# The opening of a Fourier-mixing and feed-forward kernel: some loads moved to GpSimd's queue, half a weight fold moved, one column sent and fetched half a step earlier

## The chip, the cores and the metric

The kernel runs on one core of a Trainium2 chip. A core has TensorE (matrix products, PE in the profile, PEld for its weight loads), VectorE (DVE), ScalarE (ACT), GpSimd (POOL) and SyncE (SP), each with its own instruction order, and 16 DMA engines that serve transfers issued by SyncE, ScalarE or GpSimd. An engine waits for another by semaphores. The metric is the device time of one execution in microseconds; the median of three runs before the change is 1947.78 us (1946.93 to 1948.93).

## The reference

Two stages, all in float32:

```python
def _attn_ref(x):                      # x: (8, 3008, 256)
    X = np.fft.fft(x, axis=1)
    X = np.fft.fft(X, axis=2)
    return X.real

def _moe_ref(x, w_in, w_out):          # x: (24064, 256), w_in: (256, 2048), w_out: (2048, 256)
    h = x @ w_in
    g = h * np.cos(h)
    return g @ w_out
```

The real part of a two-dimensional Fourier transform of each batch is the input of a feed-forward layer whose activation is h cos(h).

## The kernel before, in words

**The transform along the sequence.** 3008 is split as 47 x 64. `load_x` (L146) brings one batch of x into four tiles `xp`, p = 0 to 3, of eight columns i (the index of 64) together with their eight mirror columns. Each p takes four transfers, two of 32 and two of 16 partitions: the columns as they stand (L154), 8 KB in a piece, and the mirror columns in reverse order (L161), 1 KB in a piece. For p = 0 the mirror of column 0 is row 32, which is a transfer of its own (L159) beside the other seven (L156). `fold` (L248) forms sums and differences along d, and a small copy (L259) puts two border columns in place. For the first batch the folds are VectorE's and the small copies GpSimd's, into two buffers `xf` whose lower halves GpSimd clears at the start (L238). `first_half` (L274 to L291) multiplies by the table `L`, ScalarE copies the result out (L308), `store_z` (L348) writes it to DRAM and `load_z` (L358) reads it back in another layout. `second_half` (L372) multiplies by twiddles from the table `BJ` in groups g of four j; ScalarE copies the result to `pq` (L384, L387 in the first group).

**The transform along d is folded into the weights.** `weights` (L438) multiplies blocks q of 512 columns of w_in (`wr`, raw) by the cosine and sine table `CS`, two products for the two halves of the rows. VectorE copies the sums to `WC` and `WS` (L449). The first row of `WS` is used as a per-feature factor: `send_wn` (L479) writes it to DRAM (`wd`) and has GpSimd clear the row afterwards (L480), and `load_wn` (L483) fetches it as four columns of `wn`, 128 x 4 elements of 4 bytes. Block 0 takes another way (L458 to L472). `combine_w2` (L521) forms four sums and differences of blocks of w_out (`w2`) in `VX`, on GpSimd.

**The steady loop.** For 8 batches, 6 groups and 8 pairs of feature blocks there is a step t; a step has two half steps k = 2t and 2t + 1. A half step seeds a PSUM tile H from `nb` and `wn` (`seed`, L536), adds two products by WC and WS (`mm1`, L555), and goes through ScalarE and VectorE by `act_e`, `dve_h`, `act_round`, `dve_frac`, `act_sin`, `dve_g` (L567 to L597). Once a step, GpSimd forms sums `S` (L613 to L620), and seven products by w2 and VX follow (`mm2`, L646), five half steps behind the first. The next batch's transform is woven into the loop.

**The opening** is what comes before the loop runs full. Python order is issue order on every engine (the schedule is manual), and the waits are added between them. A dummy product by `keep_busy` (L502) runs on TensorE before the first data come. Then come the loads, the first batch's folds and products in the order p = 1, 2, 0, 3, the first weight folds, the first group of the second half, and half steps k = 0 to 4, in which the other weight blocks are folded between the products. Nearly all loads are SyncE's; ScalarE issues three x loads and a few small ones. Transfers of SyncE and ScalarE share eight completion semaphores in turn, so the issue of one waits until the one eight places earlier has landed. In half step 0 the first two units take their product by WC and a product with one row (`seed_first`, L542), instead of a seed by ScalarE; then `spread_nb` (L403, L404) fills `nb`:

```python
            if k == 0:
                for h in (cur, nxt):
                    mm1(h, 0)
                    seed_first(h)
                    act_e(h)
                spread_nb(0)
            if k < AHEAD - 1:
                mm1(cur, 1)
            if k == 0:
                weights(0, 1, pw=pw[0], both=(1,))
```

Of the kernel before, what the change touches and what calls it, by code (L numbers as in the profile page):

```python
# [18 lines left out]
ND = 256  # L19
# [8 lines left out]
NX = 96  # L28
# [86 lines left out]
def kernel(  # L115
# [7 lines left out]
    nc = tc.nc  # L123
    NB = x.shape[0]
    L_np, B_np, CS_np = _consts()
    L_dr = nc.inline_tensor(L_np, name="dft_L")
    ident_dr = nc.inline_tensor(np.eye(128, dtype=np.float32), name="ident")
    B_dr = nc.inline_tensor(B_np, name="dft_B")
    CS_dr = nc.inline_tensor(CS_np, name="dft_CS")

    x_r = x.rearrange("b (s2 s1) d -> b s2 s1 d", s1=64)
# [9 lines left out]
    xs = {}  # L141

    def take_x(b, p):
        xs[b, p] = spool.tile([128, XP * ND], FP, tag="xp", bufs=4, name="xp")

    def load_x(b, p, others=(nc.sync, nc.sync)):  # L146
        if (b, p) not in xs:
            take_x(b, p)
        xt = xs[b, p]
        xv = xt.rearrange("r (i d) -> r i d", d=ND)  # L150
        i0 = XP * p
        for r0, r1, at, by, other in ((0, 32, 0, 3, others[0]), (31, 47, 2, 6, others[1])):
            lo, hi = xv[at:NX:by], xv[at + by // 2 : NX : by]
            nc.sync.dma_start(out=lo, in_=x_r[b, r0:r1, i0 : i0 + XP, :])  # L154
            if p == 0:
                other.dma_start(  # L156
                    out=hi[:, 1:XP], in_=x_r[b, r0:r1, 63 : 64 - XP : -1, :]
                )
                other.dma_start(out=hi[:, 0:1], in_=x_r[b, r0:r1, 32:33, :])  # L159
            else:  # L160
                other.dma_start(  # L161
                    out=hi, in_=x_r[b, r0:r1, 64 - i0 : 64 - i0 - XP : -1, :]
                )
# [18 lines left out]
            in_=CS_dr.ap().rearrange("(i p) d -> p i d", p=128),  # L182
        )

    def load_w(q):
        nc.sync.dma_start(
            out=wr[q][:, 0:1024].rearrange("p (i f) -> p i f", i=2),
            in_=moe_w_in[:, 512 * q : 512 * q + 512].rearrange("(i p) f -> p i f", p=128),
        )

    def load_bj(c0, c1):
        nc.sync.dma_start(out=BJ[:, c0:c1], in_=B_dr.ap()[:, c0:c1])

    def load_ident():
        nc.sync.dma_start(out=ident, in_=ident_dr.ap())

    def load_w2(f0, f1):
        nc.sync.dma_start(
            out=w2.rearrange("p (q c) -> p q c", c=ND)[:, 2 * f0 : 2 * f1],
            in_=moe_w_out.rearrange("(q p) c -> p q c", p=128)[:, 2 * f0 : 2 * f1],  # L200
        )

    load_x(0, 1, (nc.scalar, nc.scalar))
    nc.sync.dma_start(out=L, in_=L_dr.ap())
    load_x(0, 2, (nc.scalar, nc.sync))
    load_x(0, 0)
    load_x(0, 3)
    load_cs()
    load_w(0)
    WC = cpool.tile([128, NDFF], FP, tag="WC", name="WC")  # L210
    WS = cpool.tile([128, NDFF], FP, tag="WS", name="WS")
    wn = cpool.tile([128, 16], FP, tag="wn", name="wn")
# [186 lines left out]
    def spread_nb(g):  # L399
        pq, nb = ready[0, g]  # L400
        T = _width(g)
        pn = borrow("pn") if g else psum("pn", "M")
        nc.tensor.matmul(pn[:, 0:T], lhsT=ones, rhs=pq[0:1, T : 2 * T], start=True, stop=True)  # L403
        nc.scalar.copy(out=nb[:, 0:T], in_=pn[:, 0:T])  # L404
# [30 lines left out]
    def weights(e, n, tag="M", pw=None, both=(0, 1)):  # L435
        pw = pw or psum("pw", tag)
        for i in both:
            nc.tensor.matmul(  # L438
                pw,
                lhsT=CS[:, 256 * i + 128 * e : 256 * i + 128 * e + 128],  # L440
                rhs=raw(n, i),
                start=(i == 0),
                stop=(i == 1),
            )
        return pw
# [30 lines left out]
    def send_wn(n):  # L476
        row = WS[0:1, 512 * n : 512 * n + 512]
        wds[n] = dpool.tile([1, 512], FP, tag="wd", bufs=3, name="wd")
        nc.scalar.dma_start(out=wds[n], in_=row)  # L479
        nc.gpsimd.memset(row, 0.0)  # L480

    def load_wn(n, eng=nc.sync):
        eng.dma_start(  # L483
            out=wn[:, 4 * n : 4 * n + 4], in_=wds[n].rearrange("o (k p) -> (o p) k", p=128)
        )
# [13 lines left out]
    def keep_busy(k, tag, n):  # L499
        pd = psum("pd", tag)  # L500
        for i in range(k):
            nc.tensor.matmul(  # L502
                pd[:, 0:n],
                lhsT=VX[:, 0:128],
                rhs=VX[:, 0:n],
                start=i == 0,
                stop=i == k - 1,
            )
# [55 lines left out]
    def act_e(h):  # L564
        T = h.s.T
        h.ew = spool.tile([128, 256], FP, tag="ew", bufs=2, name="ew")
        nc.scalar.mul(out=h.ew[:, 0:T], in_=h.H[:, 0:T], mul=2.0)  # L567
# [225 lines left out]
    both = nc.sync, nc.scalar  # L793
    copy_v = nc.vector.tensor_copy
    keep_busy(1, "H", 512)
    keep_busy(1, "H", 512)
    keep_busy(1, "M", 512)
    for p in (1, 2, 0, 3):
        for c in (2 * p, 2 * p + 1):
            chunk(c)  # L800
            first_half(0, c)
        store_z(0, p, 0, 4, both if p == 3 else (nc.sync, nc.sync))
        if p == 1:
            load_bj(0, 512)
        elif p == 2:
            load_w(1)
    load_z(0, 0, 0, 4)
    load_z(0, 1, 0, 4, both)
    fold_weights(1, 0, "H", copy_v)
# [1 line left out]
    take_wn(0)  # L811
    fold_weights(1, 1, "M", copy_v)
    send_wn(1)
    load_w2(0, 2)
    load_w(2)
    load_w(3)
    load_w2(2, 4)
    load_wn(1)
    for p in (1, 2, 0, 3):
        store_z(0, p, 4)  # L820
    load_bj(512, 1024)
    for half in range(2):
        load_z(0, half, 4)
    load_w2(4, 6)
# [37 lines left out]
    for k in range(2 * n + LAG):  # L862
        t, u = divmod(k, 2)
        d, v = divmod(k - LAG, 2)
        cur, prev, old, nxt = unit(k), unit(k - 1), unit(k - 2), unit(k + 1)
        done = step(d)
        full = step(d if v else d - 1, True)
        if cur:
            if k % (2 * per) == 0:
                todo = transform(cur.s.b + 1) if cur.s.b + 1 < NB else {}  # L870
            if k >= AHEAD:
                mm1(cur, 0)
                act_e(cur)
            if k == 0:
                for h in (cur, nxt):
                    mm1(h, 0)
                    seed_first(h)
                    act_e(h)
                spread_nb(0)
            if k < AHEAD - 1:  # L880
                mm1(cur, 1)
            if k == 0:
                weights(0, 1, pw=pw[0], both=(1,))
        pair = None if u else pairs.pop(t, None)
        if pair:
            b, c = pair
            pz = [first_half(b, c, borrow("pz"))]
        if old:
            dve_g(old)
            if old.u:  # L890
                sums(old.s)
        if pair:
            pz.append(first_half(b, c + 1, borrow("pz", 1)))
        pm = clear_middle() if u and t in middles else None
        if done:
            order = (0, 1, 5, 4, 3, 2, 6) if done is steps[-1] else range(7)
            mm2(done, 4 * v, 4 * v + 3, order)
        if pm is not None:
            middle(pm)
        if full and full is not steps[-1]:  # L900
            take_m(full, 1 if v else 3, nc.vector)
        if nxt and 0 < k < AHEAD - 1:
            seed(nxt)
        if prev:
            act_round(prev)
        if pm is not None:
            nc.scalar.copy(out=zm[64:128], in_=pm)
        if pair:
            keep_z(b, c, pz[0])
        if nxt and k >= AHEAD - 1:  # L910
            seed(nxt)
        if full and full is not steps[-1]:
            take_m(full, 0 if v else 2, nc.scalar)
        if prev:
            dve_frac(prev)
        if k + 1 in range(2, AHEAD):
            mm1(nxt, 0)
            act_e(nxt)
        if k in (1, 2, 3, 4):
            pw.append(weights(*((1, 2), (0, 2), (1, 3), (0, 3))[k - 1]))  # L920
        copy_small()
        if prev:
            act_sin(prev)
        if pair:
            keep_z(b, c + 1, pz[1])
            patch_z(b, c)
            patch_z(b, c + 1)
        if cur and k >= AHEAD - 1:
            mm1(cur, 1)
        if done and v == 0:  # L930
            mm2(done, 3, 4, order)
        if cur:
            dve_h(cur)
        if k in (1, 2, 3, 4, 5):
            e, q = ((0, 1), (1, 2), (0, 2), (1, 3), (0, 3))[k - 1]
            keep_weights(e, q, pw[k - 1], copy_v)
        if k in (3, 5):
            send_wn((k + 1) // 2)
        if k in (5, 7):
            load_wn((k - 1) // 2, nc.scalar)  # L940
        if u == 0:
            continue
        for i in range(6):
            s = step(t - 4 - i, True)
            if s:
                combine_m(s, i)
        for sg, lag in ((0, 8), (1, 10)):
            s = step(t - lag, True)
            if s:
                store_out(s, sg)  # L950
        for call in opening.pop(t, ()):
            call[0](*call[1:])
        for call in todo.pop(t % per, ()):
            call[0](*call[1:])
# [31 lines left out]
```

## Time and profile before

| What | Value |
|---|---|
| Median of three runs | 1947.78 us |
| Profiled execution, time | 1947.23 us |
| Profiled execution, span | 1945.4 us |
| TensorE busy | 1932.7 us, 99% of the span |
| VectorE, ScalarE, GpSimd busy | 1462.6, 1505.6, 1400.1 us |
| Folds of x on VectorE, first batch (L248) | 16, 676 ns each |
| First and last fold's set begin | 6.85 us, 17.82 us |
| First product of the first stage, end of that stage on TensorE | 7.95 us, 21.49 us |
| Second stage's first product (L372) | 27.89 us |
| First product with S (L646) | 47.03 us |
| TensorE gapless from | 53.05 us |
| GpSimd's first clear of xf | 0.73 us, two of them 1.84 us |

"L12" is line 12 of the kernel. A group of the profile shows line, engine, operation, what is written and read, count, busy time and mean, and then the idle time of that engine before it with what ended it. A row of the timeline begins with start and length in microseconds. Waits give the total, how many and the longest. A weight load or product is recorded as two passes per instruction in float32, so one product counts as two. "SPq", "ACTq" and "POOLq" are an engine's instruction queue, where DMAs are issued. The granted clock of TensorE is 1.00 at full speed. Idle time of an engine that nobody waits for costs nothing.

### The profile page before, as it was taken

The page shows a single profiled execution, that of the slowest core. Times are in us where ns is not written, and L with a number is a line of the kernel's source. Part 1 is how long each engine was busy: PE and PEld are TensorE (multiplying, and loading weights), DVE is VectorE, ACT ScalarE, POOL GpSimd, SP SyncE. Part 2 cuts the span into 40 slices and gives each one's busy share as a digit, 9 for nine tenths or more (in the row PEclk, how much of TensorE's full clock was granted, in tenths as well). Part 3 has the DMA queues.
Part 4 walks back from the last instruction along what each step waited for, and adds up shares of the span by engine and source line. Part 5 has one row for each costly group of instructions (what it writes and reads, how often), then busy time and mean ns, then how long its engine had stood idle before and what let it go on. Part 6 is the DMA issues. An engine that isn't in the chain of part 4 may idle for free.

```text
span 1945.4 us, 29495 instructions
## 1 busy us (share of the span) xinstructions
PE 1932.7 (99%) x9228; PEld 1682.0 (86%) x9228; DVE 1462.6 (75%) x2537; ACT 1505.6 (77%) x3439; POOL 1400.1 (72%) x1594
## 2 busy tenths in 40 slices
PE   8999999999999999999999999999999999999998
PEld 5888898888988889888898888988889888898887
DVE  4677777777777777777777777777777777788787
ACT  3777778777787777877778787788777887778775
POOL 3777757787677766787668776677767777666765
PEclk9999999999999999999999999999999999999999
DMA  8411122012220223112230112312113111100001
GB/s 212 119 28 39 28 58 72 18 39 40 54 62 19 42 41 77 36 23 40 40 90 21 39 26 41 88 24 40 24 40 87 24 39 28 39 22 16 12 14 31
DMA packets 177373, 89.09 MB, mean 46 GB/s; under 512 B 103825, under 2 KB 174271, under 8 KB 175554
## 3 DMA queue, kind: packets, MB, share of 16 engines
q1 hardware_dynamic: 174404, 86.05, 19.6%
q10 hardware_dynamic: 2814, 1.16, 0.3%
q8 instruction: 75, 1.23, 0.3%
q14 instruction: 80, 0.66, 0.1%
HBM read 49.90 MB, written 37.28 MB: 45 GB/s over the span
## 4 chain that ended last, share of the span: by engine, by line
PE 97%; DMA 2%; SPq 0%; DVE 0%; ACTq 0%; issue 0%; POOL 0%; ACT 0%; POOLq 0%; DVEq 0%
PE M L646 58%; PE H L555 33%; PE pz L277 3%; PE pb L372 2%; DMA xp<-in_x_dram 1%; DMA wn<-wd 0%; PE pw L438 0%; DMA z<-zd 0%; DMA wd<-WS 0%; DMA zd<-zs 0%; SPq L348 0%; PE pz L274 0%; PE pm L329 0%; SPq L154 0%; DVE cb L714 0%; ACTq L161 0%
## 5 line engine op out<-in xcount | busy, mean ns | idle before, releaser
L613 POOL TENSOR_TENSOR S<-r 128x512 f32<-128x512 f32 (+1 forms) x383 | 475.6, 1242 | 443.5 <-DVE r L597 392.0
L587 DVE SCALAR_TENSOR_TENSOR r<-r,H 128x512 f32<-128x512 f32 (+1 forms) x768 | 518.9, 676 | 195.2 <-ACT r L583 168.6
L593 ACT ACTIVATE r<-r 128x512 f32<-128x512 f32 (+1 forms) x768 | 477.0, 621 | 240.2 <-DVE r L587 235.5
L597 DVE SCALAR_TENSOR_TENSOR r<-H,r 128x512 f32<-128x512 f32 (+1 forms) x768 | 519.1, 676 | 131.5 <-ACT r L593 91.6
L646 PE MATMUL M<-S,VX 128*128 128x256 f32 (+1 forms) x2304 | 615.2, 376 | 0.0
L646 PEld LDWEIGHTS M<-S,VX 128*128 128x128 f32 x2304 | 435.4, 190 | 71.3 <-issue 22.7
L555 PE MATMUL H<-pq,WC 128*128 128x256 f32 (+1 forms) x1536 | 453.6, 377 | 1.4 <-ACT H L536 1.3
L555 PE MATMUL H<-pq,WS 128*128 128x256 f32 (+1 forms) x1536 | 451.3, 375 | 0.0
L583 ACT ACTIVATE r<-H 128x512 f32<-128x512 f32 (+1 forms) x768 | 447.7, 583 | 0.2 <-DVE H L571 0.2
L571 DVE TENSOR_TENSOR H<-ew,H 128x256 f32<-128x256 f32 (+1 forms) x768 | 324.9, 423 | 133.3 <-PE H L555 74.7
L646 PE MATMUL M<-r,w 128*128 128x256 f32 (+1 forms) x1536 | 387.6, 375 | 0.0
L567 ACT ACTIVATE ew<-H 128x256 f32<-128x256 f32 (+1 forms) x768 | 287.7, 375 | 123.2 <-PE H L555 119.1
L536 ACT ACTIVATE H<-nb,wn 128x256 f32<-128x256 f32 (+1 forms) x766 | 366.0, 478 | 2.7 <-DMA wn<-wd 1.8
L646 PEld LDWEIGHTS M<-r,w 128*128 128x128 f32 x1536 | 300.5, 196 | 27.5 <-issue 0.5
L555 PEld LDWEIGHTS H<-pq,WS 128*128 128x128 f32 x1536 | 290.3, 190 | 34.4 <-issue 1.5
L555 PEld LDWEIGHTS H<-pq,WC 128*128 128x128 f32 x1536 | 279.6, 190 | 45.6 <-ACT H L536 9.3
L619 POOL TENSOR_TENSOR S<-S,r 128x256 f32<-128x256 f32 (+1 forms) x383 | 276.0, 721 | 30.0
L620 POOL TENSOR_TENSOR S<-r,S 128x256 f32<-128x256 f32 (+1 forms) x383 | 275.3, 719 | 30.0
L646 PE MATMUL M<-S,w 128*128 128x256 f32 (+1 forms) x768 | 225.2, 375 | 0.0
L646 PE MATMUL M<-r,VX 128*128 128x256 f32 (+1 forms) x768 | 225.1, 375 | 0.0
L646 PEld LDWEIGHTS M<-S,w 128*128 128x128 f32 x768 | 150.5, 196 | 14.6
L646 PEld LDWEIGHTS M<-r,VX 128*128 128x128 f32 x768 | 145.8, 190 | 14.6
(76 smaller groups left out, 918.0 us busy)
## 6 DMA issues: line engine op xcount, KB each, us to landing
out_dram<-ob SPq DMA_DIRECT2D x724, 32.0 KB
xp<-in_x_dram SPq DMA_DIRECT2D x54, 256.0 KB
zd<-zs SPq DMA_DIRECT2D x56, 192.0 KB
z<-zd SPq DMA_DIRECT2D x28, 384.0 KB
xp<-in_x_dram SPq DMA_DIRECT2D x55, 128.0 KB
nb<-nd SPq DMA_DIRECT2D x39, 128.0 KB
wr<-in_moe_w_in_dram SPq DMA_DIRECT2D x4, 512.0 KB
w<-in_moe_w_out_dram SPq DMA_DIRECT2D x4, 512.0 KB
```

What stands on the lines that cost most here:

```text
L536: nc.scalar.activation(out=h.H[:, 0:T], in_=s.nb[:, 0:T], func=AF.Copy, bias=0.25, scale=wn[:, f : f + 1])
L555: nc.tensor.matmul(h.H[:, 0:T], lhsT=W[:, 128 * f : 128 * f + 128], rhs=s.pq[:, e * T : e * T + T], start=False, stop=True, skip_group_che ...
L567: nc.scalar.mul(out=h.ew[:, 0:T], in_=h.H[:, 0:T], mul=2.0)
L571: nc.vector.tensor_tensor(out=h.H[:, T : 2 * T][:, ::-1], in0=h.ew[:, 0:T], in1=h.H[:, 0:T], op=ALU.subtract)
L583: nc.scalar.activation(out=r, in_=y, func=AF.Copy, bias=BIG, scale=1.0)
L587: nc.vector.scalar_tensor_tensor(out=r, in0=r, scalar=-BIG, in1=y, op0=ALU.add, op1=ALU.subtract)
L593: nc.scalar.activation(out=r, in_=r, func=AF.Sin, bias=0.0, scale=SIN_SCALE)
L597: nc.vector.scalar_tensor_tensor(out=r, in0=y, scalar=-0.25, in1=r, op0=ALU.add, op1=ALU.mult)
L613: tt(out=sv[:, 0:2], in0=qv[:, 1:2].to_broadcast([128, 2, T]), in1=qv[:, 0:4:3], op=ALU.subtract,)
L619: tt(out=sv[:, 2], in0=sv[:, 1], in1=gv[:, 0, 0], op=ALU.subtract)
L620: tt(out=sv[:, 3], in0=gv[:, 1, 0], in1=sv[:, 2], op=ALU.add)
L646: nc.tensor.matmul(acc[key][m // 2][:, 256 * (m % 2) : 256 * (m % 2) + T], lhsT=w, rhs=a, start=first, stop=s.fp == 7, skip_group_check=True,)
```

## The change

Python lines are moved and queues changed in the opening only; the loop's later order is the same.

- `L` and row 32 of the first batch (a new `load_row`) are issued by GpSimd, ahead of its clears of `xf`. `load_x` leaves row 32 out for batch 0.
- ScalarE issues the mirror loads of p = 1 and p = 2, two each; before, SyncE had one of them.
- The weight blocks 1, 2 and 3, all `w2` blocks and all `BJ` blocks are issued by GpSimd. Block 0 and `CS` stay with SyncE. Weight block 1, the first `BJ` block, the first `w2` block and weight block 2 come behind the last small copy of the first batch on GpSimd; weight block 3, the other `w2` blocks and the other `BJ` blocks come behind the clear of `send_wn(1)`, and ahead of the first `combine_w2`.
- The second `keep_busy` dummy tile before the first data gets two products instead of one.
- The load of `wn` block 1 comes behind the eight z stores on SyncE instead of ahead of them.
- The second product of the fold (0, 1) comes between the first and the second unit of half step 0.
- `wn` block 2 is sent at k = 2 and loaded at k = 4 instead of k = 3 and 5; its clear on GpSimd is now ahead of the first sums S. Block 3 stays at k = 5 and 7.

```diff
+    def load_row(b):
+        if (b, 0) not in xs:
+            take_x(b, 0)
+        for r0, r1, at, by in ((0, 32, 1, 3), (31, 47, 5, 6)):
+            nc.gpsimd.dma_start(out=xs[b, 0][at:NX:by, 0:ND], in_=x_r[b, r0:r1, 32, :])
...
-                other.dma_start(out=hi[:, 0:1], in_=x_r[b, r0:r1, 32:33, :])
+                if b:
+                    other.dma_start(out=hi[:, 0:1], in_=x_r[b, r0:r1, 32:33, :])
...
-    def load_w(q):
-        nc.sync.dma_start(
+    def load_w(q, eng=nc.gpsimd):
+        eng.dma_start(
...
     def load_bj(c0, c1):
-        nc.sync.dma_start(out=BJ[:, c0:c1], in_=B_dr.ap()[:, c0:c1])
+        nc.gpsimd.dma_start(out=BJ[:, c0:c1], in_=B_dr.ap()[:, c0:c1])
...
     def load_w2(f0, f1):
-        nc.sync.dma_start(
+        nc.gpsimd.dma_start(
...
-    load_x(0, 1, (nc.scalar, nc.scalar))
-    nc.sync.dma_start(out=L, in_=L_dr.ap())
-    load_x(0, 2, (nc.scalar, nc.sync))
-    load_x(0, 0)
-    load_x(0, 3)
+    nc.gpsimd.dma_start(out=L, in_=L_dr.ap())
+    for p in (1, 2, 0, 3):
+        take_x(0, p)
+    load_row(0)
+    for p in (1, 2, 0, 3):
+        load_x(0, p, (nc.scalar, nc.scalar) if p in (1, 2) else (nc.sync, nc.sync))
     load_cs()
-    load_w(0)
+    load_w(0, nc.sync)
...
-    keep_busy(1, "M", 512)
+    keep_busy(2, "M", 512)
     for p in (1, 2, 0, 3):
         for c in (2 * p, 2 * p + 1):
             chunk(c)
             first_half(0, c)
         store_z(0, p, 0, 4, both if p == 3 else (nc.sync, nc.sync))
-        if p == 1:
-            load_bj(0, 512)
-        elif p == 2:
-            load_w(1)
+    load_w(1)
+    load_bj(0, 512)
+    load_w2(0, 2)
+    load_w(2)
     load_z(0, 0, 0, 4)
     load_z(0, 1, 0, 4, both)
     fold_weights(1, 0, "H", copy_v)
...
     send_wn(1)
-    load_w2(0, 2)
-    load_w(2)
     load_w(3)
     load_w2(2, 4)
-    load_wn(1)
+    load_bj(512, 1024)
     for p in (1, 2, 0, 3):
         store_z(0, p, 4)
-    load_bj(512, 1024)
+    load_wn(1)
     for half in range(2):
         load_z(0, half, 4)
     load_w2(4, 6)
     load_w2(6, 8)
     load_bj(1024, NJ * 128)
...
                     act_e(h)
+                    if h is cur:
+                        weights(0, 1, pw=pw[0], both=(1,))
                 spread_nb(0)
             if k < AHEAD - 1:
                 mm1(cur, 1)
-            if k == 0:
-                weights(0, 1, pw=pw[0], both=(1,))
...
-        if k in (3, 5):
-            send_wn((k + 1) // 2)
-        if k in (5, 7):
-            load_wn((k - 1) // 2, nc.scalar)
+        if k in (2, 5):
+            send_wn(2 if k == 2 else 3)
+        elif k in (4, 7):
+            load_wn(2 if k == 4 else 3, nc.scalar)
```

## The prediction

> **What bounds the kernel now.** I read the page's engine table and its chain first, then TensorE's waits in the first 60 us, then a table of stretches of the opening, and last the timeline of GpSimd and ScalarE there. Engine table and chain:
>
> ```profile
> PE 1932.7 (99%) x9228; PEld 1682.0 (86%) x9228; DVE 1462.6 (75%) x2537; ACT 1505.6 (77%) x3439; POOL 1400.1 (72%) x1594
> PE 97%; DMA 2%; SPq 0%; DVE 0%; ACTq 0%; issue 0%; POOL 0%; ACT 0%; POOLq 0%; DVEq 0%
> ```
>
> TensorE is busy for 1932.7 of 1945.4 us, so only 12.7 us of idle time exist. From about 53 us on it runs without a gap, and the order of instructions there is the same in both kernels, so the change can only move the moment at which that stretch begins. TensorE's waits up to 60 us:
>
> ```profile
> PE pz L277 <- POOL xf L259: 2.3, 2, 1.4
> PE pz L277 <- DMA L<-dft_L: 1.5, 1, 1.5
> PE pd L502 <- DVE VX L493: 1.5, 1, 1.5
> PE H L555 <- ACT H L536: 1.3, 1, 1.3
> ```
>
> The first product waits for L, two later first-stage products wait for folds, which wait for x, and at 51.76 us one product waits 1.3 us for a seed. The stretches (length, PE busy and instructions, granted clock, DMA share, GB/s):
>
> ```profile
> 2.00:10.50 8.50, 7.03 (x18) 1.00 1.03 255
> 10.50:13.50 3.00, 2.08 (x10) 1.00 0.56 136
> 13.50:17.60 4.10, 3.62 (x23) 1.00 0.90 247
> 29.75:33.15 3.40, 3.32 (x14) 1.00 0.98 324
> 33.15:36.55 3.40, 3.40 (x8) 0.51 0.63 152
> 36.55:39.95 3.40, 3.40 (x11) 0.99 0.68 189
> ```
>
> Two things are to be seen: the DMA engines are half empty from 10.5 to 13.5 us, while x is still awaited, and TensorE counts as busy from 33.15 to 36.55 us at half clock, a loss that no wait shows. Last, GpSimd, and the seed for which ScalarE is late:
>
> ```profile
> 18.50 0.66 POOL L259 COPY xf<-xp 96x8 f32<-96x8 f32 x1
> 33.01 0.52 POOL L480 MEMSET WS<- 1x512 f32 x1 [5.80 <-DMA wd<-WS]
> 33.58 1.41 POOL L521 TENSOR_TENSOR VX<-w 128x256 f32<-128x256 f32 x2
> 38.65 0.74 POOL L521 TENSOR_TENSOR VX<-w,VX 128x256 f32<-128x256 f32 x1
> 40.60 1.07 POOL L613 TENSOR_TENSOR S<-r 128x450 f32<-128x450 f32 x1 [1.21 <-DVE r L597]
> 52.54 0.45 ACT L536 ACTIVATE H<-nb,wn 128x225 f32<-128x225 f32 x1 [1.81 <-DMA wn<-wd]
> ```
>
> GpSimd has some 13 us free between 19.2 and 33 us, and almost none from 33 to 43 us.
>
> **The change part by part.** Times are those of the profiled execution.
>
> **x earlier.** SyncE loses L, the two row-32 loads (L159) and one second-set load; GpSimd issues L and the rows, ScalarE four x loads at 0.74 us each instead of three. Before, SyncE stands still for 2.2 + 1.4 us at L154 and L161 until an earlier x transfer is in, since a hardware-queue transfer waits for the eighth before it. After, the first two sets are the first eight, since L is none of them. x is 48 x 64 rows of 1 KB, 3.15 MB, with L 3.28 MB. At the 255 GB/s of the first stretch that is 12.9 us from 2.0 us, so the last set can land near 15.0; with some completion time I take its first fold at 15.4 instead of 17.82: 2.4 us gained. Bounds: nothing, if the queues starve again; 3.5 us, where VectorE's sixteen folds (4 x 2.48 us) run without a gap. After that point everything follows the folds: the first stage would end at 19.1 instead of 21.49.
> GpSimd now issues three DMAs before its two clears of xf (1.84 us). The first fold needs the first clear at 6.85, so up to 1.7 us an issue is hidden. The extra dummy product is two passes of 0.84 us after 6.48: TensorE is free by 8.2 instead of 7.95. The second set's folds reuse the buffer only after 9.4, so I take zero for it.
>
> **Weights and twiddles by GpSimd.** Four loads (w1, BJ, w2, w(2)) follow the last small copy, which would move from 18.50 to about 16.1. Even at 1.5 us each they are issued by 23, where GpSimd idled. They are 1.8 MB, 7 us at 255 GB/s, and share the DMA engines with the stores and loads of the first z blocks. Before, those were issued at 21.42 to 25.5 and the product at 27.89 (L372) did not wait for them; the DMA was nearly idle at 24 to 25. I take 0.3 us of new wait there, bounds 0 and 1.0 (about 256 KB more in front of them). w(3) moves from 26.6 to behind the clear that ended at 33.53, about 31.1 in the new time; its product came at 41.31, about 37.4 now. Issued by 31.9, 512 KB at half of 255 GB/s take 4.1 us: it is in by 36 and costs nothing, but only 1.4 us of cover is left.
>
> **GpSimd's block of six.** Behind that same clear, in order on GpSimd, now stand w(3), two twiddle blocks and three w2 blocks, then the eight combinations (33.58 to 39.39, 5.81 us), then the clear for column block 2, then the first sums S. No DMA issue on GpSimd is in this trace. Nearest rows: an issue on SyncE of the same loads, 0.40 to 0.47 us; ScalarE's x issue, 0.745; GpSimd's own longest pass, 1.24. TensorE needs the first S (L646) at 47.03, 25.54 us after the first stage's end, 23.8 with the clock repaired. GpSimd has the clear done 12.0 us after that end, the combinations 17.9 plus the six issues, and 1.7 us more for clear and first sum: 4.2 us of issues are free, 0.7 each. I take 0.75, the row between the two others: 4.5, so 0.3 us late. Ends: 0 at 0.40, and 3.2 us at 1.24 (7.4 - 4.2).
> [...]
>
> **Half a fold between the first products.** From 29.89 to 33.05 TensorE runs six small products 0.57 us apart, though a pair of passes at full rate takes 0.38 (L555 at 38.08 to 38.46): about two thirds filled, three of them with one row. Then the clock falls to half for 3.4 us. At full clock the half fold at 33.05 would end 0.7 us sooner (0.86 instead of 1.56), and the half step from 34.61 to 38.08 would take 2.47, as the next two do, instead of 3.47: 1.7 us together. The half fold moved into the gap fills it, at 0.86 us more for the second unit's chain (L567, L404, L536); its seed comes at 34.35 instead of 33.5, when TensorE has done two more products and would wait about 0.2. So -1.5, bounds -1.7 and +0.2.
>
> **Column block 2.** Its row is sent at k = 2, loaded at k = 4, so 2.47 us sooner; the landing took 6.15 us (46.36 to 52.52). TensorE's idle 1.3 us there would go; send and load stay two half steps apart, so ScalarE waits no longer at L483. The DMA is fuller then, as x of the next batch is no longer behind w2 on SyncE (8.37 us at L198). I take -1.1, bounds -1.3 and 0. Late next would be S on GpSimd.
>
> **Sum:** -2.4 + 0.3 + 0.3 - 1.5 - 1.1 = -4.4 us. The profiled execution took 1947.23 (span 1945.4 and 1.8 around it), 0.55 below the median of 1947.78; against the median the forecast is 1943.4.
>
> **The rivals.**
> *GpSimd becomes the bound (slower).* If one issue costs 2.2 us, the six take 13.2 and S is 9.0 late; column block 2 then hides behind it, and the sum is -2.4 + 0.3 - 1.5 + 9.0 = +5.4: 1953.2. It decides from 1.3 us each (3.6 us of gains used up). For it: three of the six carry 512 pieces of 1 KB, and GpSimd is the slowest engine for a pass of this size. Against it: no row here is above 1.24.
> *The same, milder*, at 1.0 to 1.5 us: 1.8 to 4.8 late, 1946 to 1949.
> *x lands no sooner:* the first term is zero and the time 1945.8. For it: the share is already 1.03 up to 10.5. Against it: 0.56 after that.
> [...]
> *The clock falls anyway,* because another thin stretch (a late z block, a late S) fills one window of 3.4 us, or because the stretch is met differently in each execution: 1944.9.
> [...]
>
> **How the numbers follow.** Forecast 0.54 (own range 1941.6 to 1944.4, where x is 1 us later), GpSimd bound 0.17, milder 0.11, no sooner x 0.08, clock anyway 0.10. 0.2% of 1947.78 is 3.9 us, about what a measurement of this kernel can tell from no change: faster means below 1943.9, slower above 1951.7. Faster: 0.46 of the forecast, 0.04 of the clock case, 0.01 of the x case, 0.51. Slower: 0.17. Within: 0.32. The range goes from 1941.0 (all terms at their better ends give -6.5, 1941.3) to 1950.0, past the milder case; about 0.17 lies above it and 0.03 below.
>
> **What would show it.** The last set's first fold near 15.4 and the first stage's end near 19.1; no stretch at half clock after 29 us; no wait at L536 for wn; TensorE's gapless part from about 48.5 instead of 53.05; a wait of at most 0.5 us of the first L646 products for S. A wait there of several us, with GpSimd's issues in a row before the combinations, proves me wrong; so does a wait of L372 for z or of the fourth weight block.

## The result and the profile after

The changed kernel takes 1954.47 us (median of 8 runs, 1954.15 to 1955.59), where the kernel before took 1947.58 on the same chip: a ratio of 1.0036, with a 95% interval of 1.0025 to 1.0047. It is slower by about 7 us; the prediction was 4.4 us faster. The profiled execution took 1954.44 us, span 1952.7 (before: 1947.23 and 1945.4). Line numbers after the first helper are 6 to 8 higher than before: L285 was L277, L380 was L372, L446 was L438, L544 was L536, L563 was L555.

The engine table and the shares of the chain, as shown of before:

```profile
PE 1936.1 (99%) x9230; PEld 1683.3 (86%) x9230; DVE 1461.5 (75%) x2537; ACT 1504.5 (77%) x3439; POOL 1405.3 (72%) x1607
PE 98%; DMA 1%; SPq 0%; DVE 0%; ACT 0%; issue 0%; ACTq 0%; POOL 0%; POOLq 0%; DVEq 0%
```

TensorE is busy for 3.4 us more and idle for 3.9 us more (1952.7 - 1936.1 = 16.6 against 12.7). The added dummy product is the two more instructions, and 1.35 us of it (the dummies run for 6.38 us instead of 5.03); that the rest of the same work takes 2 us longer is the first hint at the clock. TensorE's waits in the opening:

```profile
PE H L563 <- ACT H L544: 4.6, 1, 4.6
PE pb L380 <- DMA z<-zd: 3.6, 1, 3.6
PE pd L510 <- DVE VX L501: 1.5, 1, 1.5
PE pz L285 <- POOL xf L267: 1.0, 1, 1.0
```

The waits for x shrank from 3.8 us (L and two folds) to 1.0, as intended. Above them stand two new waits, each larger than any of before: one product waits for the z blocks to come back from memory, another for a seed of ScalarE. The stretches (start and end, then length, PE busy and instructions, granted clock, DMA share, GB/s); the two windows at half clock have a row each, which overlaps its neighbours:

```profile
2.00:10.50 8.50, 7.54 (x16) 1.00 1.02 253
10.50:13.50 3.00, 3.00 (x15) 1.00 1.06 264
13.50:17.60 4.10, 4.10 (x26) 1.00 1.03 297
24.40:27.80 3.40, 1.98 (x5) 1.00 0.50 162
27.80:31.20 3.40, 1.19 (x9) 0.94 0.59 164
30.70:34.10 3.40, 3.40 (x9) 0.51 0.87 205
41.40:44.80 3.40, 1.73 (x6) 1.00 0.87 316
44.80:48.20 3.40, 0.43 (x1) 0.95 1.06 203
47.75:51.15 3.40, 3.38 (x5) 0.52 1.23 190
51.20:54.60 3.40, 3.40 (x13) 0.99 1.02 193
```

From 10.5 to 17.6 us everything is better: the DMA engines are full and TensorE has no gap. Then TensorE stands twice, and behind each pause the clock falls to half for 3.4 us (from 30.79 and from 47.86 us). What the two waits wait for is in the chain of waits (start, length, what):

```profile
20.50 6.93 DMA zd<-zs
...
33.40 1.17 SPq L356
34.57 0.04 issue
34.62 12.63 DMA wn<-wd
47.24 0.02 issue
47.27 0.46 ACT H L544
```

The last z store, issued at 20.50, takes 6.93 us to land. The load of weight row block 1, 2 KB, is issued behind the eight later z stores and takes 12.63 us, counted from the start of its issue. SyncE's and GpSimd's timelines say where these stood (start, length, instruction):

```profile
27.86 6.71 SPq L356 DMA_DIRECT2D zd<-zs  x8
34.62 6.46 SPq L491 DMA_DIRECT2D wn<-wd  x1
...
17.78 0.75 POOL L193 DMA_DIRECT2D wr<-in_moe_w_in_dram  x1 [0.25 <-issue]
18.52 0.54 POOL L199 DMA_DIRECT2D BJ<-dft_B  x1
19.06 0.76 POOL L205 DMA_DIRECT2D w<-in_moe_w_out_dram  x1
19.80 0.71 POOL L193 DMA_DIRECT2D wr<-in_moe_w_in_dram  x1
```

GpSimd had put its four loads, 1.8 MB, out by 20.51, just as the last z store was issued. And the issue of the wn load itself stood for 6.46 us on SyncE.

The account, after less before, in the profiled executions: first stage ended at 19.78 instead of 21.49, -1.7; wait for z +3.6; the half-clock window near 31 to 34 us about as before, 0; wait for the row of weights +4.6; a second half-clock window from 47.9 on, half of 3.4, +1.7; the old wait for column block 2 gone, -1.3. Together +6.9 of the 7.3 by which the spans differ. The second stage's work tells the same: the product that waits for the row starts at 47.77 us, and before the same product started at 40.93.

### The profile page after: what moved, and what is told of

It reads as the page before. It is cut to its first block, busy times and chain, and to the rows that moved or that the text cites. A ratio compares the mean times of both kernels' runs of the same rounds, so it can differ in the third digit from the quotient of the medians.

```text
span 1952.7 us, 29510 instructions
## 1 busy us (share of the span) xinstructions
PE 1936.1 (99%) x9230; PEld 1683.3 (86%) x9230; DVE 1461.5 (75%) x2537; ACT 1504.5 (77%) x3439; POOL 1405.3 (72%) x1607
## 4 chain that ended last, share of the span: by engine, by line
PE 98%; DMA 1%; SPq 0%; DVE 0%; ACT 0%; issue 0%; ACTq 0%; POOL 0%; POOLq 0%; DVEq 0%
PE M L654 58%; PE H L563 33%; PE pz L285 3%; PE pb L380 2%; DMA wn<-wd 1%; DMA zd<-zs 0%; SPq L356 0%; DMA xp<-in_x_dram 0%; PE pw L446 0%; PE pz L282 0%; PE pm L337 0%; DVE cb L722 0%; PE po L752 0%; ACTq L168 0%; POOL xf L267 0%
## 5 line engine op out<-in xcount | busy, mean ns | idle before, releaser
L563 PE MATMUL H<-pq,WC 128*128 128x256 f32 (+1 forms) x1536 | 454.0, 377 | 4.6 <-ACT H L544 4.6
L563 PE MATMUL H<-pq,WS 128*128 128x256 f32 (+1 forms) x1536 | 450.9, 375 | 0.0
L544 ACT ACTIVATE H<-nb,wn 128x256 f32<-128x256 f32 (+1 forms) x766 | 366.2, 478 | 6.3 <-DMA wn<-wd 5.4
L563 PEld LDWEIGHTS H<-pq,WC 128*128 128x128 f32 x1536 | 279.9, 190 | 49.5 <-ACT H L544 13.2
L563 PEld LDWEIGHTS H<-pq,WS 128*128 128x128 f32 x1536 | 290.0, 190 | 33.9 <-issue 1.5
```

The costliest lines, as they stand in the source:

```text
L544: nc.scalar.activation(out=h.H[:, 0:T], in_=s.nb[:, 0:T], func=AF.Copy, bias=0.25, scale=wn[:, f : f + 1])
L563: nc.tensor.matmul(h.H[:, 0:T], lhsT=W[:, 128 * f : 128 * f + 128], rhs=s.pq[:, e * T : e * T + T], start=False, stop=True, skip_group_che ...
```

## The experiments

The theory at this point: the z wait and the wn wait are caused by the moved loads and by the moved row, and the other three parts (x, half fold, column block 2) are worth about what was forecast. The rival: the other parts are worth nothing, or the waits come from something common to the whole opening. Each kernel was measured against the kernel before on its own chip, on one of four chips; ratio and interval are taken over all runs and can differ a little from those of the medians.

### Taking the bytes from in front of the z stores (e1_z)

```diff
     load_w(1)
     load_bj(0, 512)
-    load_w2(0, 2)
-    load_w(2)
...
     take_wn(0)
+    load_w2(0, 2)
+    load_w(2)
```

> The kernel after, with w2 block 0 and weight block 2 issued behind the clear of WS's first row instead of ahead of the z round trip; the load of wn block 1 stays behind the z stores. Theory (GpSimd's 1.8 MB in front of the z blocks hold up their stores): only 0.8 MB are left in front, so the last z store lands in under 4 us instead of 6.9, TensorE's wait at L380 falls from 3.6 us to under 1.5, and the half-clock stretch behind it shrinks or goes; the wait for wn block 1 stays at 4 to 6 us. Time about 1951 (1949 to 1953). Rival (the stores are slow by themselves or because of the x loads before them on SyncE's queue): L380 still waits over 3 us and the time stays at 1954.

Measured: 1954.98 us, ratio 1.0031 [1.0020, 1.0043]. The step itself came out as expected, the total and the wait for the row did not. The last z store landed in 3.99 us (the chain of waits), and the wait at L380 was 0.7; the wait for the row grew to 7.4:

```profile
20.97 3.99 DMA zd<-zs
PE H L563 <- ACT H L544: 7.4, 1, 7.4
PE pb L380 <- DMA z<-zd: 0.7, 1, 0.7
```

And SyncE's timeline of the same kernel:

```profile
25.38 13.32 SPq L356 DMA_DIRECT2D zd<-zs  x8
38.74 3.92 SPq L491 DMA_DIRECT2D wn<-wd  x1
```

The eight later stores start 2.5 us sooner, but SyncE is stuck in them for 13.3 us, the row behind them lands at the same time as in the changed kernel (47.4 against 47.2), and what the first wait gave is spent in the second. The two loads were moved and not taken away: GpSimd now issues them at 26.44 and 27.19, shortly ahead of its six. The window at half clock after the z wait is gone in this profile, but after the wait of 7.4 us TensorE ran at half clock from 47.9 us, when it started again, to about 53.9.

### Loading the row ahead of the stores (e2_wn, and e3_both with both moves)

```diff
+    load_wn(1)
     for p in (1, 2, 0, 3):
         store_z(0, p, 4)
-    load_wn(1)
```

> The kernel after, with only the load of wn block 1 put back ahead of the eight z stores on SyncE. Theory (the load's issue is held up behind the stores and comes 4.6 us late): it is issued near 30 us instead of 34.6 to 41.1, lands by about 37, and neither ScalarE's 5.4 us nor TensorE's 4.6 us wait for wn block 1 is left, nor the half-clock stretch at 48 us. Time 1954.5 - 4.6 - 1.6 = 1948.3 (1947 to 1950); L380 still waits 3.6 us. Rival (GpSimd's loads make the landing slow wherever the issue stands): a wait of 3 us or more is left, time above 1951.

Measured: 1953.79 us, ratio 1.0027 [1.0017, 1.0037]. The row is issued at 30.40 and no product waits for it, so with GpSimd's six loads in flight its place behind the stores was the cause of that wait (whether the place alone would cost it, without those loads, was not run). The 4.6 us did not come out at the end, though: 1948.3 was expected. Stretches of this kernel:

```profile
27.80:31.20 3.40, 0.54 (x2) 0.77 0.14 39
31.20:34.60 3.40, 3.40 (x12) 0.50 0.73 140
34.60:38.00 3.40, 3.40 (x6) 0.50 0.97 325
38.00:41.40 3.40, 3.40 (x9) 0.50 1.05 408
41.40:44.80 3.40, 3.40 (x8) 0.50 0.79 307
44.80:48.20 3.40, 3.40 (x9) 0.72 0.68 204
```

After the pause for z (4.4 us here) TensorE stays at half clock until about 46.7 us, five windows in all: up to 8 us lost with no wait to see. Six of the seven runs have a mean granted clock of 0.995 or 0.996, as the profiled one; the seventh, at 0.998, took 1949.17, near what was expected.

Both moves together:

> Both edits: w2 block 0 and weight block 2 behind the clear of WS's first row, and the load of wn block 1 ahead of the z stores. Theory (these two waits are the whole loss): the two gains add up, 1954.5 - 3 - 6 = 1945.5 (1943.5 to 1947), below the kernel before, since x stays 1.7 us earlier and the wait for column block 2 stays away. Rival (other parts of the change cost as well): not below 1948.

Measured: 1948.79 us, ratio 1.0006 [0.9997, 1.0014]. Neither of the two waits is left, here with TensorE at full clock up to the next wait, and the kernel is back at the time of before, but not below it as the theory had it (1945.5): the rival's "not below 1948" came. One z store of the later eight takes 13.85 us (32.69 to 46.54), ScalarE's load of row block 2 waits for it, and TensorE waits 3.0 us for the seed.

### All of GpSimd's weight loads back on SyncE (e4_sync)

```diff
-    def load_w(q, eng=nc.gpsimd):
+    def load_w(q, eng=nc.sync):
...
         store_z(0, p, 0, 4, both if p == 3 else (nc.sync, nc.sync))
-    load_w(1)
-    load_bj(0, 512)
-    load_w2(0, 2)
-    load_w(2)
+        if p == 1:
+            load_bj(0, 512)
+        elif p == 2:
+            load_w(1)
...
     send_wn(1)
+    load_w2(0, 2)
+    load_w(2)
     load_w(3)
     load_w2(2, 4)
-    load_bj(512, 1024)
+    load_wn(1)
     for p in (1, 2, 0, 3):
         store_z(0, p, 4)
-    load_wn(1)
+    load_bj(512, 1024)
```

(`load_bj` and `load_w2` issue on SyncE likewise.) L, row 32, the four x loads on ScalarE, the half fold and column block 2 stay as changed.

> The kernel after, with weights, twiddles and w2 issued by SyncE again in the places they had before, and the load of wn block 1 ahead of the z stores; L, row 32, the x queues, the moved half fold and the earlier column block 2 stay. Theory (moving the weights and the wn load is the whole loss, the rest gains what was forecast for it): no wait at L380 and none for wn block 1; 1947.6 - 1.7 (x) - 1.3 (column block 2) - 0 to 1.5 (clock) = 1943 to 1945. Rival (the small parts cost too, or their gain is given back at the next wait): 1947 or more.

Measured: 1943.91 us, ratio 0.9981 [0.9972, 0.9989]: faster than before by 4 us, as expected. TensorE's waits:

```profile
PE pz L285 <- POOL xf L267: 1.5, 1, 1.5
PE pd L510 <- DVE VX L501: 1.5, 1, 1.5
PE H L563 <- ACT ew L575: 1.2, 1, 1.2
```

No stretch of the opening is at half clock in this profile. So the moved weights, with the row that moved along with them, turn a gain of 4 us into a loss of 7.

### The queue, or the bytes in front?

Two kernels start from the last one. In the first, the four loads w1, BJ, w2 block 0 and w(2) are issued by SyncE ahead of the last z store; in the second, by GpSimd where the changed kernel has them. The six later loads stay on SyncE in both.

```diff
-        if p == 1:
-            load_bj(0, 512)
-        elif p == 2:
-            load_w(1)
+        if p == 0:
+            load_w(1)
+            load_bj(0, 512)
+            load_w2(0, 2)
+            load_w(2)
...
     send_wn(1)
-    load_w2(0, 2)
-    load_w(2)
     load_w(3)
```

> The kernel of e4_sync, but the four loads w1, BJ, w2 block 0 and w(2), 1.8 MB, stand ahead of the last z store on SyncE, as many bytes as GpSimd had put in front of it. If the z round trip is slow because of the bytes in front, whatever the queue, the last store takes about 7 us again, the product at L380 waits 3 to 4 us, and the time is 1947 to 1949. If it is slow because GpSimd's software queue carries them, the store lands within 4 us, the wait is under 1 us, and the time is 1944 to 1945.

Measured: 1950.22 us, ratio 1.0018 [1.0009, 1.0027]; the wait is as expected, the time 1.2 us above the range, as TensorE also waits 2.0 us for row block 2. The second:

> The kernel of e4_sync, but the same four loads by GpSimd, in the changed kernel's place (behind the last first-stage copies); the later six stay on SyncE and the load of wn block 1 ahead of the z stores. If the first block of GpSimd's loads costs by itself, L380 waits 3.6 us for z as in the changed kernel, one stretch of 3.4 us at half clock follows (1.7 us), nothing waits for wn, and the time is 1943.9 + 5.3 = 1949.2. If it needs both blocks, or if the slack behind it takes it up, the time is 1944 to 1946.

Measured: 1949.82 us, ratio 1.0022 [1.0013, 1.0030]. The last z store in the chain of waits of e9_four_hw, with SyncE's loads in front:

```profile
20.55 6.17 DMA zd<-zs
```

And in the chain of e10_four_sw, with GpSimd's:

```profile
20.56 6.74 DMA zd<-zs
```

```profile
PE pb L380 <- DMA z<-zd: 3.4, 1, 3.4
```

TensorE waits those 3.4 us at L380 in both. A suspicion formed after the first runs, that GpSimd's software queue is what starves the z stores, falls for this block: the bytes in front decide, whoever issued them. With the same 1.8 MB in front the store took 6.17 us where SyncE had issued them and 6.74 where GpSimd had.

For the block of six the same pair of kernels was made. By GpSimd in a row, with the row ahead of the stores:

```diff
     load_w2(0, 2)
     load_w(2)
-    load_w(3)
-    load_w2(2, 4)
+    load_w(3, nc.gpsimd)
+    load_w2(2, 4, nc.gpsimd)
+    load_bj(512, 1024, nc.gpsimd)
     load_wn(1)
     for p in (1, 2, 0, 3):
         store_z(0, p, 4)
-    load_bj(512, 1024)
...
-    load_w2(4, 6)
-    load_w2(6, 8)
-    load_bj(1024, NJ * 128)
+    load_w2(4, 6, nc.gpsimd)
+    load_w2(6, 8, nc.gpsimd)
+    load_bj(1024, NJ * 128, nc.gpsimd)
```

> The kernel of e4_sync, but GpSimd issues the last six loads (w(3), three blocks of w2, two of the twiddles) in a row before its combinations, as in the changed kernel; the first loads stay on SyncE and the load of wn block 1 ahead of the z stores. If the six put 4 MB in front of the later z stores, those stores take 13 to 15 us instead of 6.5, ScalarE's load of wn block 2 stands behind them, TensorE waits about 3 us and the time is 1947 to 1949, as with e3_both. If the block of six costs only GpSimd's 4 us of issues, which the S sums have room for, it is 1944 to 1945.

Measured: 1948.47 us, ratio 1.0004 [0.9995, 1.0012], in the expected range, but by another wait: the eight stores do take 14.73 us, and it is the later z block that comes back late (2.9 us at L380, at 56.78 us), not the row. By SyncE ahead of the row and the stores:

> The kernel of e4_sync, but the six loads that GpSimd had issued in a row stand ahead of wn block 1 and the eight later z stores on SyncE. If the bytes in front delay the stores, whatever the queue, the row of wn block 1 and the stores land 8 us or more later than in e4_sync (there the stores were done by 38.7 us), TensorE waits 3 us or more for wn or z, and the time is 1947 or above. If only GpSimd's queue does it, the time is within 0.5 us of e4_sync's 1943.9.

Measured: 1945.46 us, ratio 0.9994 [0.9985, 1.0002], which is neither answer. By medians it is 1.4 us below before on its chip, where e4_sync is 4.1 below on another; the intervals overlap. TensorE waits 2.1 us for row block 1, which is issued behind the six and lands at 39.6. SyncE's timeline of e11_six_sw, with GpSimd's six:

```profile
29.70 14.73 SPq L356 DMA_DIRECT2D zd<-zs  x8
```

And of e14_six_hw, with SyncE's:

```profile
32.39 0.37 SPq L491 DMA_DIRECT2D wn<-wd  x1
32.80 9.47 SPq L356 DMA_DIRECT2D zd<-zs  x8
```

SyncE spends 6.4 us on the issues of the eight stores in the kernel before, where two of the six loads went out 6 us ahead and four behind (33.38, 6.38), 9.5 with SyncE's six in front and 14.7 with GpSimd's. SyncE had its six out by 29.7 us, GpSimd began only at 29.9 and overlapped the stores wholly. Queue and moment are not separated here, so for this block the part of the queue stays open.

### The three other parts

Each was put alone on the kernel before. The half fold:

```diff
                     act_e(h)
+                    if h is cur:
+                        weights(0, 1, pw=pw[0], both=(1,))
...
-            if k == 0:
-                weights(0, 1, pw=pw[0], both=(1,))
```

> The kernel before with nothing changed but the place of the half fold (weights(0, 1, both=(1,)) moved from the end of half step 0 to behind act_e of its first unit). If the thin stretch of six small products is what drops the clock, the stretch at 0.51 from 33.15 to 36.55 us is gone, the gapless part begins some 1.5 us sooner and the time is 1946.5 (before: 1948.0). If the clock falls for another reason, a window of 3.4 us at half rate is still there near 33 us and the time stays at 1948.0, within 0.4.

Measured: 1947.73 us against 1946.79, ratio 1.0004 [0.9995, 1.0013]: no gain, though its profile has full clock throughout the opening. The x part, with `load_row` and `load_x` as changed:

```diff
-    load_x(0, 1, (nc.scalar, nc.scalar))
-    nc.sync.dma_start(out=L, in_=L_dr.ap())
-    load_x(0, 2, (nc.scalar, nc.sync))
-    load_x(0, 0)
-    load_x(0, 3)
+    nc.gpsimd.dma_start(out=L, in_=L_dr.ap())
+    for p in (1, 2, 0, 3):
+        take_x(0, p)
+    load_row(0)
+    for p in (1, 2, 0, 3):
+        load_x(0, p, (nc.scalar, nc.scalar) if p in (1, 2) else (nc.sync, nc.sync))
...
-    keep_busy(1, "M", 512)
+    keep_busy(2, "M", 512)
```

> The kernel before with the first part of the change alone: L and the row-32 loads by GpSimd, four x loads by ScalarE, two dummy products; weights, twiddles and rows of the weights as before. The changed kernel's first stage ended 1.7 us sooner (19.78 instead of 21.49). If that is passed on, and the half-clock stretch of before stays, the time is 1946.3; by the forecast's 2.4 us it would be 1945.6. If the gain is lost again where the loads behind x on SyncE still land as before, the time is 1948.0.

Measured: 1946.19 us, ratio 0.9995 [0.9987, 1.0004]: about 1 us, not told from none. Column block 2:

```diff
-        if k in (3, 5):
-            send_wn((k + 1) // 2)
-        if k in (5, 7):
-            load_wn((k - 1) // 2, nc.scalar)
+        if k in (2, 5):
+            send_wn(2 if k == 2 else 3)
+        elif k in (4, 7):
+            load_wn(2 if k == 4 else 3, nc.scalar)
```

> The kernel before with nothing changed but the row of column block 2 sent at half step 2 and loaded at 4 (3 and 5 before). In the profile of before TensorE waits 1.3 us at L536 for it. If that wait goes and nothing takes its place, the time is 1.1 to 1.3 us below before. If the load of block 3 on ScalarE's queue or the S sums are late next, it is within 0.4 us of before.

Measured: 1946.81 us, ratio 0.9997 [0.9988, 1.0006]. The wait at 51.8 us is gone, and the row of block 3 is late in its place: TensorE waits 1.7 us at 60.74, at the same line of the code. Last, the kernel of e4_sync without the half fold's move:

```diff
-                    if h is cur:
-                        weights(0, 1, pw=pw[0], both=(1,))
...
+            if k == 0:
+                weights(0, 1, pw=pw[0], both=(1,))
```

> The kernel of e4_sync with the half fold back at the end of half step 0, where the kernel before has it. By the forecast's term one window of 3.4 us at half clock comes back near 30 us and the time is 1.5 us longer, 1945.4. If the move of the half fold is worth nothing, as e5_half alone measured, it is 1943.9.

Measured: 1944.54 us, ratio 0.9989 [0.9980, 0.9998]. Its opening from 27 to 60 us ran at full clock, with the thin stretch of six small products in its old place. Against before on its own chip it gains 2.6 us by medians, e4_sync 4.1 on another chip, and e12_best below, on the same chip, 3.0: the half fold would be worth 0.4 to 1.5 us, and the intervals overlap.

### The last column block

> The kernel of e4_sync with the load of wn block 3 on ScalarE's queue one half step later (8 instead of 7), so that ScalarE does not stand for 2.0 us until the row has landed. TensorE's wait of 1.2 us at L563 for ew goes: 1942.7. If another wait takes its place, 1943.9 as e4_sync.

```diff
-        elif k in (4, 7):
+        elif k in (4, 8):
```

Measured: 1944.11 us, ratio 0.9981 [0.9972, 0.9990], the same as e4_sync: the wait of 1.2 us went and one of 0.9 for block 3's seed came. Sending that row a half step sooner:

```diff
-        if k in (2, 5):
-            send_wn(2 if k == 2 else 3)
-        elif k in (4, 7):
+        if k in (4, 7):
             load_wn(2 if k == 4 else 3, nc.scalar)
+        if k in (2, 4):
+            send_wn(2 if k == 2 else 3)
```

> The kernel of e4_sync with the row of column block 3 sent at half step 4 instead of 5 and loaded at 7. In e4_sync ScalarE stands for 2.0 us at that load and TensorE 1.2 us behind it; in e12_best (loaded at 8) TensorE waits 0.9 us for the seed of block 3. If both waits go: 1942.9. If another one takes their place: 1943.9.

Measured: 1944.54 us, ratio 0.9986 [0.9977, 0.9995]. Now S on GpSimd is 1.9 us late. Three places in a row for one or two microseconds of wait: the opening seems limited there by several chains of nearly the same length. The best version is the kernel of e4_sync (or e12_best), 0.19% faster than before.

## Why the prediction was wrong

**The step that failed** is "I take 0.3 us of new wait there, bounds 0 and 1.0 (about 256 KB more in front of them)". Measured: 3.6 us, with a z store of 6.93 us. The right number stood two sentences earlier: "1.8 MB, 7 us at 255 GB/s". I set those 7 us beside the idle DMA of 24 to 25 us in the old order, instead of asking what is in front of the last z store in the new one. All four loads were issued before it (17.78 to 20.51, store at 20.50), so nearly all of their 7 us was in front. With no weight load in front (before) the store was issued at 22.14 and the loads that wait for it went on at 24.27; 768 KB in front (e1_z) gave 3.99 us, all of it, by either queue, 6.2 to 6.9. That this costs is shown by e1_z, which removes the wait, and by e9_four_hw and e10_four_sw, which bring it back.

**A step that was left out.** The row of wn block 1 moves from ahead of the eight z stores to behind them on SyncE. The prediction's part by part does not price it at all. It cost 4.6 us: e2_wn puts it back and no product waits for it. The timeline of before would have told: row block 1 left at 32.97, the seed was needed at 39.76 and a landing of such a row (block 2) took 6.15 us there, so by that estimate it had under 1 us to spare; the issues of the eight stores behind which it went take 6.38.

**The clock** (-1.5 forecast) gave nothing in the changed kernel. A window of half clock came at 30.8 to 34.2, now behind the pause for z, and a second from 47.9 to 51.3, behind the pause for the row. The rival that the clock falls anyway came true twice, each time just behind a pause (3.6 and 4.6 us); that a thin stretch is what drops it was my estimate, not shown. But the term was too large from the start: some executions of before have the half-clock window and others do not. Of the 115 runs of before beside the experiments, 75 had a mean granted clock of 0.999 or more and 40 had 0.998 or less, as the profiled one had; on each chip the first kind is 1.2 to 2.0 us shorter by medians, about one window. The split is rough, since the mean is rounded and e7_x has one such window at 0.999, but the forecast took from every run what only a part of them lose. Nor does the thin stretch always drop the clock: e6_col and e13_no_half keep it in its place, and their profiles are at full clock there. Whether the half fold helps at all stays open. Alone it gave nothing; but with the rest as in e4_sync (also e12_best, e14_six_hw, e15_col3) 4 of 44 runs have 0.998 or less, and without it (e13_no_half) 4 of 11, which is a hint and no more.

**Right in their steps:** x, 1.7 of 2.4 us (19.78 for a forecast 19.1; the first fold itself began later, 8.01 against 6.85, for a reason that no run takes apart); an issue on GpSimd, 0.54 to 0.76 us for the 0.75 taken; S on GpSimd not late (the first sum done at 47.41, needed at 55.66, since TensorE was later still); w(3) hidden; column block 2's wait gone. One sign came true and meant nothing: TensorE was without a gap from 47.77, near the 48.5 named, but starting at a product that the kernel before reached at 40.93. "Late next would be S on GpSimd" was right only after a further step; block 3's row came first.

**The sum of the three good parts** was forecast at -5.0 us (-2.4, -1.5, -1.1) and is -4.1 by medians in e4_sync. Alone they measure about -1.0, +0.8 and -0.6 by their ratios, each within its interval of nothing. Their profiles suggest why little comes out alone: half fold and x leave waits of 2.0 and 1.5 us for row block 2, column block 2 leaves 1.7 for block 3.

**The rival on the other side** named 1953.2, close to the measured time, and by the wrong mechanism: an issue on GpSimd took 0.54 to 0.76 us and not the 2.2 it assumed, for which it had no row, and TensorE never waited for S. What I named as proving me wrong, "a wait of L372 for z", is what came.

## What to carry to other kernels

When loads are moved to an idle queue, list for every small transfer on the critical path what is issued before it in the new order, and take bytes in front divided by the rate of that stretch as its delay (here 1.8 MB at 255 GB/s, 7 us, and the z store behind them took 6.93); an idle queue is not an idle DMA engine (the z store took 6.74 us behind GpSimd's four loads and 6.17 behind SyncE's). Price every line of a diff that changes place, a 2 KB load too: one that goes behind eight stores inherits their time (here its issue began 6.8 us after theirs, and it landed 12.63 us later). A loss of the clock seen in one profile is worth its share of the executions only (40 of 115 runs of before had 0.998 or less), and a half-clock stretch can come again behind a new pause (after 3.4 us it did in e10_four_sw's profile, 0.83 and 0.67 in the slices from 27.8 to 34.6 us, and not in e9_four_hw's, 1.00 in both).

## What the runs showed of the hardware

- Behind a pause of TensorE more can be lost than the pause, and not the same in each run: in e2_wn's profile half clock followed a pause of 4.4 us until about 46.7 us, up to 8 us lost. The kernel of e10_four_sw has a pause of 3.4 us for z in its profile; its runs, 1948.03 to 1954.60 us, order themselves by the mean granted clock:

```
clock 0.999          1948.03  1948.39  1948.58
clock 0.998          1948.96  1949.11  1949.82
clock 0.996          1951.76  1952.88
clock 0.995          1953.58  1953.66  1954.60
```

The profiled execution of the changed kernel has half clock from 30.79 to 34.21 and from 47.86 to 51.27 us, that of before from 33.19 to 36.60: 3.41 us each time, and the first two begin 17.07 us or five times 3.41 apart. One such window loses 1.7 of some 1950 us, 0.0009 of the mean. That the runs of one kernel differ by how many such windows they have is an estimate from the clocks above. Why some runs stay at half clock for five windows, through stretches in which TensorE has no gap (e2_wn), these runs do not settle.

- A DMA issue can stand: SyncE's issue of a 2 KB load took 6.46 us behind eight stores of 160 KB (the changed kernel), and 0.38 ahead of them (e2_wn).
- Packets differ by queue. In the DMA table of the changed kernel from 20.5 to 27.5 us (queue, packets, MB, share of the engines):

```profile
q0 software_dynamic: 443, 1.55, 66.9%
q1 hardware_dynamic: 360, 0.16, 9.0%
```

GpSimd's packets (q0) carry 3.5 KB each, those of SyncE's z store and loads (q1) 0.44 KB, and in that stretch the small ones carry a tenth of the bytes. That this is why the six loads on GpSimd's queue stretched the stores to 14.7 us is an argument, not shown.
